# One head's last K tile taken in halves, and the output weights loaded wholly behind V, in a one-core decode kernel

## The chip, the cores and the metric

The kernel runs on one core of a Trainium2 chip. The metric is device time in microseconds; the figure for a kernel is the median of its runs.

## The reference

One token goes through cached attention and through a gated feed-forward network (FFN), and a gate mixes the two. There are 32 heads of 128 dimensions with 65536 keys each, the model width is 512 and the FFN's hidden width 1792. All inputs are bf16.

```python
x = A_x
g = _sigmoid((x * gate_w).sum(-1, keepdims=True))
# attention, per head h: q = x @ wq, p = softmax(q . k_cache[h] / sqrt(128)), o = p @ v_cache[h]; a = o @ wo
a = _A_ref(x, A_k_cache, A_v_cache, A_wq, A_wo)
# FFN: (silu(x @ w_gate) * (x @ w_up)) @ w_down
b = _B_ref(x, B_w_gate, B_w_up, B_w_down)
return g * a + (1 - g) * b
```

The K and V caches are 537 MB each, and each value is used once.

## The kernel before, in words

**Tiles.** A tile is 16384 keys of a head: 128 partitions with 128 keys of 128 values each (4 MB). Four tiles make a head, so there are 128 tiles of K and as many of V; they are numbered n = 0 to 127. Two tiles make a pair, numbered m = 0 to 63, which one transfer of 8 MB loads in most of the kernel. There are two K buffers of a pair each (`K_bufs`, used in turn) and one V buffer of a pair (`V_buf`), so a V pair can be loaded only after the value matmuls of the pair before it are done.

**Scores.** For a K tile, the vector engine DVE multiplies the keys in place by the query (`product`, L281) and adds the two halves of each key's 128 products (`add_halves` with `WIDE`, or `add_once`; L293 and L304). PE sums the 64 columns that are left: 16 matmuls of 512 columns against the identity (`scores`, L508) accumulate four partial sums per key in a PSUM bank (`S_ps`, one of two). DVE adds the four (`fold`, L315). In the long loop the second tile of each pair is added further on DVE, down to 16 columns (`T_sb`). When a head's four tiles are folded, DVE takes the maximum per partition (`row_max`, L321), PE and DVE find the maximum of all (`max_turn` L524, `top_of` L325), and ScalarE takes the exponentials of a pair at a time (`P_sb`).

**Values.** PE multiplies the exponentials with V, four keys of a partition per matmul: 32 matmuls per tile (`values`, L531). `head_turn` (L539) brings the result into one column per head, and ScalarE writes it, scaled, into `oT`. At the end `project` (L548) multiplies `oT` with `wo`: two matmuls of 256 columns per head, into `a_ps`.

**Order.** There is no scheduler: each engine's instructions stand in the order in which the code gives them, with hand-written semaphore waits. The sync engine (SP or SyncE) issues all large transfers from one queue and waits, between them, for the buffers that they overwrite.

**The prologue** (`prologue`) loads wq, then the first two K pairs (the first as two tiles), the FFN's gate and up weights, and, into places of `V_buf` that come free, the down weights; then the third K pair (L630, when tile 1's scores are done), the first V pair (L655, when the FFN's down projection has been read from `V_buf`) and the fourth K pair (L666, when tile 3's scores are done). DVE works on tiles 0 to 3, the first head; FFN work is put between them. After tile 2's add DVE waits for ScalarE's exponential of the FFN's gate (`eg`, L636), does four small operations on it, the last of which writes `hT`, and goes on to tile 3's product. On PE, in order: tile 2's scores, the 14 matmuls of the down projection from `hT` (L643), two matmuls that open `a_ps` with the FFN's part (L651), the spread of the second head's query (L521), tile 3's scores.

**The end** (`sync_end`, `tensor_end`). SP loads, after the last pair of head 30's V, the first 16 heads' rows of wo (2 MB, `EARLY`) into the first half of K buffer 0, then the last head's four V tiles: N-4 into the second half of K buffer 0, N-3 and N-2 into the V buffer's halves in two pieces each, N-1 into the second half of K buffer 1 in six pieces (`LAST_CUTS`), and then wo's other 16 heads into the first half of K buffer 1 in five pieces (`LATE_CUTS`). Heads below `GROUPED` (28) lie in rows of 4 KB, four heads to a row; heads 28 to 31 in rows of 1 KB. PE projects heads 0 to 15 in two portions around the `head_turn` of head 30, ahead of the last head's values, and heads 16 to 31 piece by piece behind them. The last 8 keys of a partition in the last tile (`TURNED`) go straight into the head's column (L745), so that `head_turn` of the last head only adds to it. Head 31's column is waited for ahead of its own two matmuls. DVE and ScalarE copy a half each of the result out, and SP stores it.

Of the kernel before, what the change touches and what calls it, by code (L numbers as in the profile page):

```python
# [8 lines left out]
ALU = mybir.AluOpType  # L9
AXIS = mybir.AxisListType  # L10
P = 128
NB = 128
PAIR = 2 * NB
QUAD = 4


WIDE = 64
WIDTH = 16

TURNED = 8  # L20
EARLY = 16
LATE_CUTS = (EARLY, 20, 24, 28, 30, 32)
HALVES = (0, 64, NB)
LAST_CUTS = (0, 32, 64, 96, 112, NB - TURNED, NB)

# [16 lines left out]
def kernel(  # L42
# [14 lines left out]
    nc = tc.nc  # L57
# [3 lines left out]
    _, H, Sk, Dh = A_k_cache.shape  # L61
    D = A_x.shape[2]
# [8 lines left out]
    HD = D // 2  # L71
# [13 lines left out]
    K_bufs = [ring.tile([P, PAIR * Dh], bf16, name=f"K{i}_buf") for i in range(2)]  # L85
# [9 lines left out]
    ident_b, ones_b, q_diag = (sb(n, [P, P], bf16) for n in ("ident_b", "ones_b", "q_diag"))  # L95
# [33 lines left out]

    K_half, V_half = [halves(b) for b in K_bufs], halves(V_buf)  # L130

    wo_sb = [b[:, : H * D].rearrange("p (h n) -> p h n", n=D) for b in K_bufs]

    def v_view(n):
        return {N - 4: K_half[0][1], N - 3: V_half[0], N - 2: V_half[1], N - 1: K_half[1][1]}[n]
# [17 lines left out]
        for n in ("x_in", "gw_in", "wq_in", "ka_in", "kb_in", "kc_in", "wg_in", "wu_in", "wd_in", "vA_in", "vB_in")  # L153
# [2 lines left out]
    v4_in = Events(nc, "v4_in", 16)  # L156
    end_in = {n: [Events(nc, f"end{n}_{i}", 16) for i in range(len(c) - 1)]
              for n, c in ((N - 3, HALVES), (N - 2, HALVES), (N - 1, LAST_CUTS))}
    wo_in = {a: Events(nc, f"wo{a}", 16) for a in (0, *LATE_CUTS[:-1])}

    c_S = [nc.alloc_semaphore(f"c_S{i}") for i in range(2)]
    c_q, c_P, c_V, c_o, c_m = (nc.alloc_semaphore(n) for n in ("c_q", "c_P", "c_V", "c_o", "c_m"))
# [5 lines left out]
    def wait(engine, events, value):  # L168
        key = id(engine), id(events)
        value -= taken.get(key, 0)  # L170
        if seen.get(key, 0) < value:
            engine.wait_ge(events.sem, value)
            seen[key] = value
# [12 lines left out]
        events(sync.dma_start(out=view[:, a:b, :], in_=rows_of(cache, n)[:, start + a : start + b, :]))  # L186

    def load_wo(a, b):
        runs = wo_sb[a >= EARLY].rearrange("p (g j) n -> p g (j n)", j=QUAD)
        rows = A_wo.rearrange("(h p) n -> p h n", p=P)  # L190
        row_runs = A_wo.rearrange("(g p j) n -> p g (j n)", p=P, j=QUAD)
        if b <= GROUPED:
            A, B = a // QUAD, b // QUAD
            wo_in[a](sync.dma_start(out=runs[:, A:B, :], in_=row_runs[:, A:B, :]))
        else:
            wo_in[a](sync.dma_start(out=wo_sb[1][:, a:b, :], in_=rows[:, a:b, :]))


    def load_v(i):
# [20 lines left out]

    def sync_end():
        wait(sync, pe_D, 6)
        load_wo(0, EARLY)
        load_tile(v_view(N - 4), A_v_cache, N - 4, v4_in)
        for n in (N - 3, N - 2, N - 1):
            if n < N - 1:
                wait(sync, pe_V, n - 2)
            else:
                wait(sync, pe_D, 8)
            cuts = LAST_CUTS if n == N - 1 else HALVES  # L230
            for events, a, b in zip(end_in[n], cuts[:-1], cuts[1:]):
                load_tile(v_view(n), A_v_cache, n, events, a, b)
        for a, b in zip(LATE_CUTS[:-1], LATE_CUTS[1:]):
            load_wo(a, b)

    def sync_out():
# [23 lines left out]

    own = [dv]

    def product(n):
        K = K_half[n // 2 % 2][n % 2]
        q = q_sb[n // G % 2]
        q_rep = bass.AP(tensor=q.tensor, offset=q[:, :].offset, ap=[list(q[:, :].ap[0]), [0, NB], [1, Dh]])
        m = n // 2

        if m == 0:
            wait(dve, (ka_in, kb_in)[n], 16)  # L270
        elif m == 1:
            wait(dve, kc_in, 16)
        elif n == N - 1:
            wait(dve, kb_in, 32)
        else:
            wait(dve, k_in[m % 2], 16 * (m // 2))
        if n < G:
            wait(dve, ac, marks["q"])
        else:
            wait(dve, ac_q, n // G)  # L280
        return own[0](dve.tensor_tensor(out=K, in0=K, in1=q_rep, op=ALU.mult))  # L281

    def add_halves(n, width, last, out=None, ahead=None):
        K = K_half[n // 2 % 2][n % 2]
        half, mark = Dh // 2, last
        while half >= width:
            wait(dve, own[0], mark)
            to = K[:, :, 0:half]
            if half == width and ahead is not None:
                fold(ahead)  # L290
            if half == width and out is not None:
                to = out
            ins = dve.tensor_tensor(out=to, in0=K[:, :, 0:half], in1=K[:, :, half : 2 * half], op=ALU.add)  # L293
            if half == width and out is not None:
                ins.then_inc(c_S[n % 2], 1)
            else:
                mark = own[0](ins)
            half //= 2
        marks["K", n] = mark

    def add_once(n, last):
        wait(dve, own[0], last)
# [200 lines left out]
        pe.wait_ge(credit, 1)  # L503
        pe.sem_inc(credit, -1)  # L504

    def scores(n, src, width, events):
        for c in range(0, width, QUAD):
            ins = pe.matmul(  # L508
                S_ps[n % 2], lhsT=ident_b, rhs=src[:, :, c : c + QUAD],
                start=(c == 0), stop=(c == width - QUAD),  # L510
            )
            if c == 0 and events is pe_S and n == 1:
                pe_K(ins)
        events(ins)

    def scores_direct(n):
        wait(pe, dv, marks["K", n])
        scores(n, K_half[n // 2 % 2][n % 2], WIDE, pe_D)

    def query_spread(events):  # L520
        events(pe.matmul(qb, lhsT=ones_b, rhs=q_diag, start=True, stop=True))  # L521
# [23 lines left out]
    def project(lo, hi):  # L545
        for h in range(lo, hi):
            for i, a in enumerate(a_ps):
                ins = pe.matmul(  # L548
                    a, lhsT=oT[:, h : h + 1], rhs=wo_sb[h >= EARLY][:, h, i * HD : (i + 1) * HD],
                    start=False, stop=(h == H - 1),  # L550
                )
                if h == H - 1:
                    pe_x(ins)


    def prologue():
# [76 lines left out]
        fold(1)  # L633
        add_halves(2, WIDE, last)
        scores_direct(2)
        wait(dve, ac, marks["eg"])  # L636
        wait(dve, dv, dv(dve.tensor_scalar_add(eg, eg, 1.0)))
        wait(dve, dv, dv(dve.reciprocal(eg, eg)))
        wait(dve, dv, dv(dve.tensor_tensor(out=hprod, in0=gu_sb[:, :FT], in1=eg, op=ALU.mult)))
        wait(pe, wd_in, 16)  # L640
        wait(pe, dv, dv(dve.tensor_tensor(out=hT, in0=hprod, in1=gu_sb[:, FT:], op=ALU.mult)))
        for t in range(FT):
            ins = pe.matmul(  # L643
                b_ps, lhsT=hT[:, t : t + 1], rhs=wd_sb[:, t, :], start=(t == 0), stop=(t == FT - 1)
            )
        pe_x(ins)
        wait(act, dv, marks["rest"])
        wait(act, pe_x, 4)
        wait(pe, ac, ac(copy(b_sb, b_ps, rest[0:1, :])))
# [8 lines left out]
        query_spread(pe_q0)  # L658
        wait(act, pe_q0, 2)
        ac_q(copy(q_sb[1], qb))  # L660
        last = product(3)
        fold(2)
        add_halves(3, WIDE, last)
        scores_direct(3)
        wait(sync, pe_D, 4)
        load_k(3)  # L666
        row_max(0, fold(3))
# [29 lines left out]
    def tensor_end():  # L697
        lower = P_sb[:, NB:]
        take(c_P)
        total()  # L700
        scores_direct(N - 4)
        take(c_V)
        pe_V(values(P_sb, V_half[0], 0, NB, True, False))
        scores_direct(N - 3)
        pe_V(values(lower, V_half[1], 0, NB, False, True))
        take(c_q)
        query_spread(pe_q)
        take(c_o)
        head_turn()
        take(c_m)  # L710
        max_turn()

        take(c_P)
        total()
        scores_direct(N - 2)
        take(c_V)
        pe_V(values(P_sb, V_half[0], 0, NB, True, False))
        scores_direct(N - 1)
        take(c_V)
        values(lower, V_half[1], 0, NB // 2, False, False)  # L720
        take(c_m)
        max_turn()
        pe_V(values(lower, V_half[1], NB // 2, NB, False, True))
        wait(pe, wo_in[0], 16)
        project(0, EARLY // 2)
        take(c_o)
        head_turn()
        project(EARLY // 2, EARLY)
        wait(pe, ac, marks["P_last"])
        wait(pe, v4_in, 16)  # L730
        pe_V(values(P_last, v_view(N - 4), 0, NB, True, False))
        for n in range(N - 3, N):
            probs = P_last[:, n % G * NB : (n % G + 1) * NB]
            cuts = LAST_CUTS if n == N - 1 else HALVES
            for events, a, b in zip(end_in[n], cuts[:-1], cuts[1:]):
                wait(pe, events, 16)
                if n == N - 1 and a == NB - TURNED:
                    break
                ins = values(probs, v_view(n), a, b, False, n == N - 1 and b == NB - TURNED)
            pe_V(ins)  # L740
            if n == N - 2:
                total(1)
        wait(pe, ac, marks["oh_read"])
        for j in range(NB - TURNED, NB):
            pe.matmul(  # L745
                oh, lhsT=v_view(N - 1)[:, j, :], rhs=probs[:, j : j + 1],
                start=(j == NB - TURNED), stop=False,
            )
        for a, b in zip(LATE_CUTS[:-1], LATE_CUTS[1:]):
            wait(pe, wo_in[a], 16)  # L750
            if a == EARLY:
                project(a, a + QUAD)
                wait(pe, ac, marks["O_last"])
                head_turn(opens=False)
                project(a + QUAD, b)
            elif b == H:
                project(a, H - 1)
                wait(pe, ac, marks["oT"])
                project(H - 1, H)
            else:  # L760
                project(a, b)

    with tc.tile_critical():
        prologue()
# [53 lines left out]
```

## Time and profile before

| | |
|---|---|
| median of 3 runs | 2520.32 us (2519.13 to 2520.52) |
| the profiled execution: its own time | 2520.22 us |
| its span, first to last instruction | 2518.4 us |
| mean granted TensorE clock | 0.774 |
| PE busy | 1485.8 us (59%) |
| DVE busy | 2003.5 us (80%) |
| ACT busy | 182.5 us (7%) |
| bytes read | 1087.64 MB, 432 GB/s over the span |

The profile is of one execution. Its views are a page (busy shares, the span in 40 slices, DMA queues, the costliest groups of instructions) and answers of the trace: timelines by engine, windows, waits. Times are microseconds from the first instruction. A timeline row gives the start, the length, the engine (SPq is SP's queue of transfers), the line of the kernel, the operation, the tiles written and read with shapes, a count, and in brackets how long the engine had been idle before and what released it. The rows of windows give start and end, the length, busy time and instruction count of PE, PE's weight loads, DVE, ACT and POOL, then the granted TensorE clock, the busy share of the 16 DMA engines, and GB/s. A large transfer is recorded in packets that are counted where they start, so a short window can show a share over 1 or of 0 although the engines are busy; windows are read together. "Time to landing" is from a transfer's issue to the event that all of its data are there.

### The profile page before, as it was taken

What the parts mean: (1) busy time and instruction counts of PE and PEld (TensorE: products, weight loads), DVE (VectorE), ACT (ScalarE), POOL (GpSimd) and SP (SyncE); (2) the same over time, 40 slices, a digit from 0 to 9 for tenths busy, and PEclk for the clock granted to TensorE, in tenths of its full rate; (3) what the DMA queues carried; (4) which work ended last, traced back from release to release, by engine and by line L of the source; (5) the groups of instructions that cost most, each with busy time, mean ns of one, the idle gap of its engine ahead of it and who ended that gap; (6) DMA issues with size and microseconds to landing.
All of it is one profiled execution on the core that took longest, in us unless ns stands there. A gap on an engine that the chain in (4) does not pass through costs nothing. (4 is left out here: it accounts for less than half of the span.)

```text
span 2518.4 us, 15666 instructions
## 1 busy us (share of the span) xinstructions
PE 1485.8 (59%) x6573; PEld 615.6 (24%) x6573; DVE 2003.5 (80%) x676; ACT 182.5 (7%) x503; POOL 0.7 (0%) x6
## 2 busy tenths in 40 slices
PE   2655646557556566465565564655755646557568
PEld 1322222222222222222222222222212222222223
DVE  5887877977878878779788787787887877977881
ACT  0000000000000000000000000000000000000000
POOL 0000000000000000000000000000000000000000
PEclk8777778778777787787787777877877778778789
DMA  9999999999999999999999999999999999999999
GB/s 413 424 432 432 433 433 433 434 433 434 433 433 433 433 433 435 439 438 434 433 433 434 434 433 433 433 433 433 433 435 438 438 434 434 433 434 434 433 429 388
DMA packets 22541, 1087.80 MB, mean 432 GB/s; under 512 B 2689, under 2 KB 3202, under 8 KB 4482
## 3 DMA queue, kind: packets, MB, share of 16 engines
q1 hardware_dynamic: 22242, 1087.65, 99.8%
q8 instruction: 7, 0.11, 0.0%
q10 hardware_dynamic: 288, 0.00, 0.0%
q14 instruction: 4, 0.03, 0.0%
HBM read 1087.64 MB, written 0.00 MB: 432 GB/s over the span
## 5 line engine op out<-in xcount | busy, mean ns | idle before, releaser
L281 DVE TENSOR_TENSOR K_buf<-K_buf,q_sb 128x16384 bf16<-128x16384 bf16 x128 | 1111.9, 8687 | 344.1 <-DMA K_buf<-in_A_k_cache_dram 344.1
L508 PE MATMUL S_ps<-K_buf,ident_b 128*128 128x512 bf16 x1088 | 387.2, 531 | 866.7 <-PEq L504 829.5
L531 PE MATMUL O_ps<-V_buf,P_sb 128*4 128x512 bf16 x3968 | 866.8, 379 | 31.8 <-PEq L504 31.4
L531 PEld LDWEIGHTS O_ps<-V_buf,P_sb 128*4 128x4 bf16 x3968 | 332.9, 85 | 563.3 <-issue 60.8
L293 DVE TENSOR_TENSOR K_buf<-K_buf 128x8192 bf16<-128x8192 bf16 (+1 forms) x128 | 438.2, 3423 | 3.1
L508 PEld LDWEIGHTS S_ps<-K_buf,ident_b 128*128 128x128 bf16 x1088 | 132.5, 126 | 1099.6 <-issue 1029.2
L304 DVE TENSOR_TENSOR K_buf<-K_buf 128x8192 bf16<-128x8192 bf16 x60 | 265.5, 4425 | 2.0
L387 ACT ACTIVATE O_sb<-O_ps 4x512 f32<-4x512 f32 x63 | 63.3, 1005 | 1705.2 <-PE qm_ps L521 1671.0
L315 DVE TENSOR_REDUCE S_sb<-S_ps 128x128 f32<-128x512 f32 x128 | 88.2, 689 | 110.3 <-PE S_ps L508 108.3
L524 PE MATMUL qm_ps<-diag,ones_f 128*128 128x128 f32 x126 | 34.0, 357 | 72.4 <-PEq L504 70.3
L539 PE MATMUL oh_ps<-ident_f,O_sb 4*128 4x1 f32 x504 | 64.3, 244 | 18.8 <-PEq L504 18.8
L293 DVE TENSOR_TENSOR T_sb<-K_buf 128x2048 bf16<-128x2048 bf16 x60 | 72.9, 1215 | 0.0
L539 PEld LDWEIGHTS oh_ps<-ident_f,O_sb 4*128 4x128 f32 x504 | 60.7, 186 | 48.7 <-issue 48.7
L508 PE MATMUL S_ps<-T_sb,ident_b 128*128 128x512 bf16 x240 | 64.7, 391 | 0.0
L524 PEld LDWEIGHTS qm_ps<-diag,ones_f 128*128 128x128 f32 x126 | 21.9, 218 | 76.7 <-issue 76.7
L387 ACT ACTIVATE bias<-top 128x1 f32<-128x1 f32 x32 | 6.5, 203 | 436.7 <-DVE top L325 436.7
L527 PE MATMUL tot_ps<-rs,ones_f 128*128 128x2 f32 (+1 forms) x126 | 24.5, 264 | 18.1 <-PEq L504 18.1
L387 ACT ACTIVATE oT<-whole_o,rg 32x1 f32 (+1 forms) x115 | 33.8, 294 | 4.7
L412 ACT ACTIVATE P_sb<-S_sb,bias 128x256 bf16<-128x256 f32 x62 | 31.5, 508 | 1.0
L527 PEld LDWEIGHTS tot_ps<-rs,ones_f 128*128 128x128 f32 x126 | 20.1, 200 | 36.9 <-issue 36.9
L334 DVE RECIPROCAL recip<-tot_ps 128x1 f32<-128x1 f32 x1 | 0.2, 169 | 32.0 <-PE tot_ps L527 32.0
L508 PEld LDWEIGHTS S_ps<-T_sb,ident_b 128*128 128x128 bf16 x240 | 20.7, 96 | 15.9
(61 smaller groups left out, 214.5 us busy)
## 6 DMA issues: line engine op xcount, KB each, us to landing
K_buf<-in_A_k_cache_dram SPq DMA_DIRECT2D x4, 4096.0 KB, 32.9
V_buf<-in_A_v_cache_dram SPq DMA_DIRECT2D x2, 4096.0 KB, 21.6
V_buf<-in_A_v_cache_dram SPq DMA_DIRECT2D x4, 2048.0 KB, 23.1
V_buf<-in_A_wq_dram SPq DMA_DIRECT2D x1, 4096.0 KB, 12.3
K_buf<-in_A_v_cache_dram SPq DMA_DIRECT2D x1, 4096.0 KB, 34.7
K_buf<-in_A_v_cache_dram SPq DMA_DIRECT2D x3, 1024.0 KB, 28.3
K_buf<-in_A_wo_dram SPq DMA_DIRECT2D x1, 2048.0 KB, 25.5
V_buf<-in_B_w_gate_dram SPq DMA_DIRECT2D x1, 1792.0 KB, 54.5
```

The costliest lines, as they stand in the source:

```text
L281: return own[0](dve.tensor_tensor(out=K, in0=K, in1=q_rep, op=ALU.mult))
L293: ins = dve.tensor_tensor(out=to, in0=K[:, :, 0:half], in1=K[:, :, half : 2 * half], op=ALU.add)
L304: dve.tensor_tensor(out=K[:, :, 0:half], in0=K[:, :, 0:half], in1=K[:, :, half:], op=ALU.add).then_inc(c_S[0], 1)
L315: return own[0](dve.tensor_reduce(out=S_sb[h % 2][:, g * NB : (g + 1) * NB], in_=S_ps[n % 2], axis=AXIS.X, op=ALU.add))
L334: wait(dve, own[0], own[0](dve.reciprocal(recip[:, 0:1], total)))
L387: return act.activation(out=out, in_=in_, func=ACT.Copy, scale=scale)
L412: return act.activation(out=out, in_=S_sb[h % 2][:, b * PAIR : b * PAIR + count], func=ACT.Exp, bias=bias[:, 0:1], scale=scale, accum_out= ...
L508: ins = pe.matmul(S_ps[n % 2], lhsT=ident_b, rhs=src[:, :, c : c + QUAD], start=(c == 0), stop=(c == width - QUAD),)
L524: pe.matmul(mT, lhsT=ones_f, rhs=diag, start=True, stop=True).then_inc(pe_m.sem, n)
L527: pe_t(pe.matmul(tot[:, :n], lhsT=ones_f, rhs=rs[:, :n], start=True, stop=True))
L531: ins = pe.matmul(O_ps, lhsT=probs[:, j : j + 4], rhs=view[:, j : j + 4, :], start=(opens and j == start), stop=(closes and j == stop - 4),)
L539: ins = pe.matmul(oh, lhsT=O_sb[:, c * Dh : (c + 1) * Dh], rhs=ident_f[0:4, c : c + 1], start=(opens and c == 0), stop=(c == 3),)
```

## The change

In the prologue, tile 3 of the first head is handled in two halves of 64 keys per partition. DVE's product of the first half stands ahead of the wait for the FFN gate's exponential, and its add behind the four gate operations; the second half's product, `fold(2)` and the second half's add follow. PE makes the first half's scores (16 matmuls of 256 columns) behind the down projection, ahead of the matmuls that open `a_ps`, and the second half's at the place where the whole tile's were. The event of tile 3's scores comes with the second half.

At the end, SP no longer loads 2 MB of wo ahead of the last head's V. All of wo (4 MB) goes into the first half of K buffer 0, behind V's last piece, in ten pieces (`WO_CUTS`): seven of four heads, one of two, two of one. PE has no projection ahead of the last head's values any more: it projects piece by piece behind them, with the last head's `head_turn` behind the first piece; the wait for head 31's column stands ahead of the last piece, which is that head alone.

```diff
-EARLY = 16
-LATE_CUTS = (EARLY, 20, 24, 28, 30, 32)
+WO_CUTS = (0, 4, 8, 12, 16, 20, 24, 28, 30, 31, 32)
...
-    wo_sb = [b[:, : H * D].rearrange("p (h n) -> p h n", n=D) for b in K_bufs]
+    wo_sb = K_bufs[0][:, : H * D].rearrange("p (h n) -> p h n", n=D)
...
     def sync_end():
         wait(sync, pe_D, 6)
-        load_wo(0, EARLY)
         load_tile(v_view(N - 4), A_v_cache, N - 4, v4_in)
...
-        for a, b in zip(LATE_CUTS[:-1], LATE_CUTS[1:]):
+        for a, b in zip(WO_CUTS[:-1], WO_CUTS[1:]):
             load_wo(a, b)
...
-    def product(n):
-        K = K_half[n // 2 % 2][n % 2]
+    def product(n, start=0, stop=NB):
+        K = K_half[n // 2 % 2][n % 2][:, start:stop, :]
...
+    def add_some(n, last, start, stop):
+        wait(dve, own[0], last)
+        K, half = K_half[n // 2 % 2][n % 2][:, start:stop, :], Dh // 2
+        marks["K", n] = own[0](dve.tensor_tensor(
+            out=K[:, :, 0:half], in0=K[:, :, 0:half], in1=K[:, :, half:], op=ALU.add
+        ))
...
-    def scores(n, src, width, events):
+    def scores(n, src, width, events, start=0, stop=NB):
         for c in range(0, width, QUAD):
             ins = pe.matmul(
-                S_ps[n % 2], lhsT=ident_b, rhs=src[:, :, c : c + QUAD],
+                S_ps[n % 2][:, start:stop, :], lhsT=ident_b, rhs=src[:, start:stop, c : c + QUAD],
...
-        events(ins)
+        if stop == NB:
+            events(ins)
...
         scores_direct(2)
+
+        first_half = product(3, 0, NB // 2)
         wait(dve, ac, marks["eg"])
...
         wait(pe, dv, dv(dve.tensor_tensor(out=hT, in0=hprod, in1=gu_sb[:, FT:], op=ALU.mult)))
+        add_some(3, first_half, 0, NB // 2)
...
         pe_x(ins)
+        scores_direct(3, 0, NB // 2)
         wait(act, dv, marks["rest"])
...
-        last = product(3)
+        last = product(3, NB // 2, NB)
         fold(2)
-        add_halves(3, WIDE, last)
-        scores_direct(3)
+        add_some(3, last, NB // 2, NB)
+        scores_direct(3, NB // 2, NB)
         wait(sync, pe_D, 4)
...
         pe_V(values(lower, V_half[1], NB // 2, NB, False, True))
-        wait(pe, wo_in[0], 16)
-        project(0, EARLY // 2)
         take(c_o)
         head_turn()
-        project(EARLY // 2, EARLY)
         wait(pe, ac, marks["P_last"])
...
-        for a, b in zip(LATE_CUTS[:-1], LATE_CUTS[1:]):
+        for a, b in zip(WO_CUTS[:-1], WO_CUTS[1:]):
             wait(pe, wo_in[a], 16)
-            if a == EARLY:
-                project(a, a + QUAD)
+            if b == H:
+                wait(pe, ac, marks["oT"])
+            project(a, b)
+            if a == 0:
                 wait(pe, ac, marks["O_last"])
                 head_turn(opens=False)
-                project(a + QUAD, b)
-            elif b == H:
-                project(a, H - 1)
-                wait(pe, ac, marks["oT"])
-                project(H - 1, H)
-            else:
-                project(a, b)
```

More of the change, by code (lines that the diff above doesn't have):

```diff
@@ L158 @@
               for n, c in ((N - 3, HALVES), (N - 2, HALVES), (N - 1, LAST_CUTS))}
-    wo_in = {a: Events(nc, f"wo{a}", 16) for a in (0, *LATE_CUTS[:-1])}
+    wo_in = {a: Events(nc, f"wo{a}", 16) for a in WO_CUTS[:-1]}
     c_S = [nc.alloc_semaphore(f"c_S{i}") for i in range(2)]
@@ L188, in load_wo @@
     def load_wo(a, b):
-        runs = wo_sb[a >= EARLY].rearrange("p (g j) n -> p g (j n)", j=QUAD)
+        runs = wo_sb.rearrange("p (g j) n -> p g (j n)", j=QUAD)
         rows = A_wo.rearrange("(h p) n -> p h n", p=P)
@@ L195, in load_wo @@
         else:
-            wo_in[a](sync.dma_start(out=wo_sb[1][:, a:b, :], in_=rows[:, a:b, :]))
+            wo_in[a](sync.dma_start(out=wo_sb[:, a:b, :], in_=rows[:, a:b, :]))
     def load_v(i):
@@ L261 @@
     own = [dv]
-    def product(n):
-        K = K_half[n // 2 % 2][n % 2]
+    def product(n, start=0, stop=NB):
+        K = K_half[n // 2 % 2][n % 2][:, start:stop, :]
         q = q_sb[n // G % 2]
-        q_rep = bass.AP(tensor=q.tensor, offset=q[:, :].offset, ap=[list(q[:, :].ap[0]), [0, NB], [1, Dh]])
+        q_rep = bass.AP(tensor=q.tensor, offset=q[:, :].offset, ap=[list(q[:, :].ap[0]), [0, stop - start], [1, Dh]])
         m = n // 2
@@ L513, in scores, with scores_direct @@
                 pe_K(ins)
-        events(ins)
-    def scores_direct(n):
+        if stop == NB:
+            events(ins)
+    def scores_direct(n, start=0, stop=NB):
         wait(pe, dv, marks["K", n])
-        scores(n, K_half[n // 2 % 2][n % 2], WIDE, pe_D)
+        scores(n, K_half[n // 2 % 2][n % 2], WIDE, pe_D, start, stop)
     def query_spread(events):
@@ L548, in project @@
                 ins = pe.matmul(
-                    a, lhsT=oT[:, h : h + 1], rhs=wo_sb[h >= EARLY][:, h, i * HD : (i + 1) * HD],
+                    a, lhsT=oT[:, h : h + 1], rhs=wo_sb[:, h, i * HD : (i + 1) * HD],
                     start=False, stop=(h == H - 1),
```

## The prediction

> **What bounds the kernel now.** I read the DMA view first: if the transfer engines never rest, only bytes or a hole in their stream can move the time.
>
> The DMA part of the page, 40 slices of 63 us:
>
> ```profile
> DMA  9999999999999999999999999999999999999999
> GB/s 413 424 432 432 433 433 433 434 433 434 433 433 433 433 433 435 439 438 434 433 433 434 434 433 433 433 433 433 433 435 438 438 434 434 433 434 434 433 429 388
> ...
> q1 hardware_dynamic: 22242, 1087.65, 99.8%
> q8 instruction: 7, 0.11, 0.0%
> ```
>
> One queue moves 1087.65 MB at some 433 GB/s from end to end. At that rate the bytes alone need 2512 us of the 2518.4. DVE (80% busy) and PE (59%) have slack, so an edit of the compute pays only where it closes a hole in the stream, or shortens what comes before the first byte or after the last. Only the first two slices and the last are under the plateau. Next, therefore, SyncE's rows (it issues all the big loads) and narrow windows of the start:
>
> ```profile
> 57.79 0.33 SPq L182 DMA_DIRECT2D K_buf<-in_A_k_cache_dram  x1
> 78.06 0.33 SPq L182 DMA_DIRECT2D V_buf<-in_A_v_cache_dram  x1
> 89.36 0.33 SPq L182 DMA_DIRECT2D K_buf<-in_A_k_cache_dram  x1
> 123.68 0.33 SPq L182 DMA_DIRECT2D V_buf<-in_A_v_cache_dram  x1
> ```
>
> Windows (the last two columns are DMA share and GB/s):
>
> ```profile
> 121.00:122.00 1.00, 1.00 (x7) 0.36 (x5) 0.27 (x1) 0.00 (x0) 0.00 (x0) 1.00 0.45 197
> 122.00:123.00 1.00, 1.00 (x6) 0.40 (x5) 0.00 (x0) 0.00 (x0) 0.00 (x0) 1.00 0.01 0
> 123.00:124.00 1.00, 1.00 (x8) 0.48 (x6) 0.00 (x0) 0.00 (x0) 0.00 (x0) 1.00 0.00 0
> ```
>
> There is one hole, from 122 to 124.6 us. The fourth K pair has run out and the second V pair is issued only at 123.68, because V has one buffer and the first V pair's 64 value matmuls (13.97 us from 109.68) end then. No other stretch up to the last byte shows such a hole. So the chain that ends in those value matmuls costs time. I followed it back on DVE:
>
> ```profile
> 62.37 4.42 DVE L293 TENSOR_TENSOR K_buf<-K_buf 128x8192 bf16<-128x8192 bf16 x1
> 69.12 0.18 DVE L637 TENSOR_SCALAR eg<-eg 128x14 f32<-128x14 f32 x1 [2.33 <-ACT eg L628]
> ...
> 69.91 8.69 DVE L281 TENSOR_TENSOR K_buf<-K_buf,q_sb 128x16384 bf16<-128x16384 bf16 x1
> ...
> 89.36 0.69 DVE L315 TENSOR_REDUCE S_sb<-S_ps 128x128 f32<-128x512 f32 x1 [5.84 <-PE S_ps L508]
> 90.09 0.69 DVE L321 TENSOR_REDUCE m<-S_sb 128x1 f32<-128x512 f32 x1
> 90.69 8.68 DVE L281 TENSOR_TENSOR K_buf<-K_buf,q_sb 128x16384 bf16<-128x16384 bf16 x1
> ```
>
> Two rests lie on the chain: 2.33 us for the FFN's exponential, and 5.84 us in which PE makes the last tile's scores. Last, the end, PE and then DVE:
>
> ```profile
> 2510.92 1.03 PE L548 MATMUL a_ps<-K_buf,oT 128*1 128x256 bf16 x8 [0.31 <-DMA K_buf<-in_A_wo_dram]
> 2511.89 1.05 PE L539 MATMUL oh_ps<-ident_f,O_sb 4*128 4x1 f32 x8
> 2512.86 2.78 PE L548 MATMUL a_ps<-K_buf,oT 128*1 128x256 bf16 x24
> 2515.57 0.41 DVE L383 CAST out_sb<-a_ps 1x256 bf16<-1x256 f32 x1 [11.50 <-PE a_ps L548]
> ```
>
> The last wo piece lands at 2500.2 + 14.5 = 2514.7 (issue plus time to landing), yet the output copy starts 0.85 us later, since PE is still in its run of 24 projection matmuls.
>
> **The change, the start.** By the order listing, DVE does: add of tile 2, product of tile 3's keys 0-63, the four gate operations, add of that half, product of keys 64-127, fold(2), add of the second half.
> Per operation, start to start, a whole product is 8.60 us, a whole add 4.34, a fold 0.60, the gate operations 0.79; halves of the first two are taken as 4.30 and 2.17. From the add's end at 66.7: first product to 71.0, gate to 71.8, add to 74.0, product to 78.3, fold to 78.9, add to 81.1, where before it ended at 83.45. DVE gains its rest, 2.35 us; nothing is added but some 0.1 us for two more instructions.
> The gate operations end 1.9 us later (71.8 for 69.9). Behind hT on PE are the 14 down-projection matmuls, which start at 74.85 anyway, after tile 2's scores: covered by 3 us, so the first V load (waiting for them at 78.06) doesn't move.
> PE then makes the first half's scores, 16 matmuls of 256 columns, from 78.06. Before these, 256 columns were only seen with a one-column weight (0.119 us each); 512 columns against the same weights took 0.227 at clock 1.0 and 0.43 at 0.5. So 16 cost between 1.8 and 6.9 us; I take 2 to 3.5, near half the 512-column price, as the stream sets it. Queued behind them are the two a_ps openers and the spread of query 1 (1.3 us together, with their ACT copy): they move from 78.9 to some 81, and query 1 is first read by tile 4's product.
> The second half's scores: from 81.2 for 2 to 3.5 us (bounds 1.8 and 6.9), so 83.2 to 84.8 (88.1 at worst) for 89.36 before. SyncE's load of the fourth K pair goes out with it; the queue is full then, so that is worth nothing by itself. Then fold and row maximum, 1.3 us. Now the next thing is late: tile 4's product waits for its K pair, which lands at 57.79 + 27.7 = 85.5. It starts at 85.5 to 86.2 for 90.69: 4.5 to 5.2 us earlier. Scores of tile 4 then start at 98.7 to 99.4 for 103.98, and, at the half clock in which they begin, end near 105.5. The first V pair lands at 78.06 + 26.7 = 104.8. So the value matmuls run from 105.6 to 119.6, and the second V pair is issued near 119.6, 2.5 us ahead of the dry queue; data followed an issue at 123.68 by 1 us (first packets at 124.64), so 1.5 us is spare.
> What the hole is worth: in the trace's packets thirteen of the sixteen DMA engines end the K pair by 122.3 and three at 123.5 to 123.8; all start again at 124.64 and the first packets take some 3.2 us for 2.42. The slowest engine's loss is the spacing of landings, 145.3 - 124.2 = 21.1 us for 19.3 between later pairs: 1.8. The first engine's is longer: its packets end at 122.27 and 144.9, so 22.6 less 19.3: 3.3. Each of the three late engines was held up by one 16 KB instruction packet (queue 8), and the hole lets the others wait for them. Which engine is last at the end differs from those, as far as lateness shows there (a 1.7 us spread after three further such packets), so I take 3.0. Later, V issues come 3.5 us ahead of the dry queue (199.37 against 202.9), so no new hole follows.
>
> **The change, the end.** SyncE no longer issues wo's first 2 MB ahead of V; V lands 4.87 us earlier against the stream, wo's last byte as before: the bytes are the same. PE loses 32 projection matmuls (2 x 1.91 us) between its value blocks and gets all 64 behind V. Value blocks of 32 take 6.72 us, and V arrives at 9.7 us a block: PE ends V at about 2505.3 in old times, and wo's pieces come 1.21 to 1.24 us apart (landings of the three 512 KB pieces) against 0.95 us for eight matmuls. PE catches up after the head turn (1.0 us) by the sixth piece. At the last piece only two matmuls are left: the copies start near 2515.25 for 2515.57. Worth 0.3 us. The five added DMAs: 0.02 us each for 512 KB pieces (1.23 for 1.21 by bytes), 0.1 for the 1 KB rows of heads 28 to 31 (0.70 for 0.60 by bytes): 0.1 in all, counted in that 0.3. Bounds: -0.3 to +0.6.
> The Trainium skill (DMA: Bandwidth & Descriptors, Anatomy of one DMA) gives a fixed cost of about 2.0 us per DMA beside the bytes, and its rules for kernel authors ask for 1 MiB or more per DMA; by that, unhidden, the cut would cost 10 us, while the rows just named show 1.23 us between whole 512 KB pieces.
>
> Sum: 3.0 + 0.3 = 3.3 us. Span 2518.4 to 2515.1; the profiled execution 2520.22 to 2516.9; the median stands 0.1 above it: **2517.0**.
>
> **The rivals.**
> *The late engine stays late (17%).* If the engine that ends last is one of the three held up at the start, only the 1.8 comes back: with the tail's 0.3, 2518.2. For it: lateness persists for hundreds of us when no hole evens it out. Against it: only some of 16 engines.
> *The hole stays (8%).* If scores at half clock take the 512-column price, or the clock comes late in the value matmuls, the V issue is not before 122 and the start gives little: 2520.0 with the tail's 0.3.
> *PE becomes the bound of the end (slower, 3%).* The place is the 64 projection matmuls behind V. They fall behind the pieces when eight cost over 1.21 us, that is at a granted clock under 0.79. At 0.5 each takes 0.107 us more, 6.8 in all: less the 3.3, 2523.8; if the last V tile's 30 matmuls run so too (0.21 more each) 2530. Against it: the clock is 1.0 from 2453 to the end, with waits of over 1 us in it, and PE's longest new wait is 1.4 us. In the Trainium skill (TensorE: Matmul & The Clock Gate, Part 1) the clock halves after an idle window of about 3.4 us, which no wait here reaches; the trace's clock fell at 128.9 after PE went idle near 127.5, so it can be quicker.
> *The pieces pay their start each (slower, 2%).* If a piece's fixed time is not hidden by the one ahead, each of five costs about the 2.1 us of the 1 KB load of x (page, part 6): 10.5 - 3.3, so 2527.5. It decides only when the queue is empty between pieces; SyncE issued the last ones 14.5 us ahead.
> That the edit doesn't do what it says is out for the order of instructions, which is listed as described.
>
> **How the numbers follow.** The forecast has 70%, 2517.0, its own range 2516 to 2518. The 80% range takes in the late engine with 0.6 us of spread between runs (2519.13 to 2520.52 before): 2515.8 to 2519.1; the hole that stays and the slower cases are left out. About 0.2%, 5.0 us, is what a measurement here can tell from no change. Faster by that would need 1.7 us more than forecast, over the hole's and the tail's bounds together (3.3 + 0.6): 3%. Slower by that: the pieces, and the clock's worse half: 4%. The rest, 93%, is within.
>
> **What would show it.** Right: no DVE wait at the gate; the 5.84 us rest under 4; tile 4's product ending a wait for DMA near 85.5; the second V pair issued near 119.6; no window without bytes near 122; copies 0.5 us after the last wo landing; the span 3 us shorter. Wrong: a V issue after 121.3; a wait on PE for wo shorter than expected with matmuls of 0.21 us; wo pieces more than 1.3 us apart.

## The result and the profile after

The changed kernel takes 2516.34 us (median of 22 runs, 2515.96 to 2518.0) where the kernel before, run beside it, takes 2520.23 (22 runs, 2518.9 to 2521.85): 3.9 us less, ratio 0.9985 with a 95% interval of 0.9979 to 0.9990. The forecast was 2517.0. The profiled execution took 2517.20 us, 0.9 above the median, with a span of 2515.4.

First the stream, from the page of the changed kernel; then SyncE's rows and the three windows around the hole of before, of which 122 to 124 us had no bytes then (columns as in the windows of the prediction):

```profile
GB/s 414 438 433 436 435 434 434 434 434 434 435 434 434 434 434 434 435 436 435 435 435 434 437 434 435 435 434 437 435 434 434 434 434 434 434 435 434 434 431 387
```

```profile
57.58 0.33 SPq L181 DMA_DIRECT2D K_buf<-in_A_k_cache_dram  x1
77.86 0.33 SPq L181 DMA_DIRECT2D V_buf<-in_A_v_cache_dram  x1
83.26 0.33 SPq L181 DMA_DIRECT2D K_buf<-in_A_k_cache_dram  x1
119.12 0.33 SPq L181 DMA_DIRECT2D V_buf<-in_A_v_cache_dram  x1
```

```profile
121.00:122.00 1.00, 0.80 (x8) 0.74 (x7) 0.00 (x0) 0.23 (x2) 0.00 (x0) 1.00 0.92 393
122.00:123.00 1.00, 0.75 (x4) 0.51 (x4) 0.00 (x0) 0.77 (x3) 0.00 (x0) 1.00 1.65 655
123.00:124.00 1.00, 0.00 (x0) 0.00 (x0) 0.00 (x0) 0.00 (x0) 0.00 (x0) 1.00 0.46 197
```

The second slice went from 424 to 438 GB/s, and the first and last stand as they did. The second V pair is issued at 119.12 us for 123.68, while the fourth K pair is still landing, so bytes move through 122 to 124. The pair after the hole now lands 24.2 us after its issue, at 143.3, 19.3 us behind the K pair (83.26 + 40.7 = 124.0), which is the distance of undisturbed pairs; before it was 21.1.

DVE of the changed kernel, from tile 2's add to tile 4's product:

```profile
62.38 4.42 DVE L291 TENSOR_TENSOR K_buf<-K_buf 128x8192 bf16<-128x8192 bf16 x1
66.72 4.42 DVE L279 TENSOR_TENSOR K_buf<-K_buf,q_sb 128x8192 bf16<-128x8192 bf16 x1
71.05 0.17 DVE L645 TENSOR_SCALAR eg<-eg 128x14 f32<-128x14 f32 x1
...
71.83 2.28 DVE L302 TENSOR_TENSOR K_buf<-K_buf 128x4096 bf16<-128x4096 bf16 x1
74.03 4.42 DVE L279 TENSOR_TENSOR K_buf<-K_buf,q_sb 128x8192 bf16<-128x8192 bf16 x1
...
83.27 0.69 DVE L320 TENSOR_REDUCE S_sb<-S_ps 128x128 f32<-128x512 f32 x1 [2.02 <-PE S_ps L513]
83.99 0.69 DVE L326 TENSOR_REDUCE m<-S_sb 128x1 f32<-128x512 f32 x1
85.41 8.69 DVE L279 TENSOR_TENSOR K_buf<-K_buf,q_sb 128x16384 bf16<-128x16384 bf16 x1 [0.73 <-DMA K_buf<-in_A_k_cache_dram]
```

The gate's operations no longer wait, the rest for PE is 2.02 us for 5.84, and tile 4's product ends a wait for its K pair at 85.41, 5.3 us earlier than before. The end, PE and DVE:

```profile
2503.29 1.03 PE L554 MATMUL a_ps<-K_buf,oT 128*1 128x256 bf16 x8 [0.21 <-DMA K_buf<-in_A_wo_dram]
2504.26 1.05 PE L545 MATMUL oh_ps<-ident_f,O_sb 4*128 4x1 f32 x8
2505.24 2.79 PE L554 MATMUL a_ps<-K_buf,oT 128*1 128x256 bf16 x24
2508.23 1.03 PE L554 MATMUL a_ps<-K_buf,oT 128*1 128x256 bf16 x8 [0.21 <-DMA K_buf<-in_A_wo_dram]
...
2510.73 1.91 PE L554 MATMUL a_ps<-K_buf,oT 128*1 128x256 bf16 x16 [0.21 <-DMA K_buf<-in_A_wo_dram]
```

```profile
2512.56 0.41 DVE L388 CAST out_sb<-a_ps 1x256 bf16<-1x256 f32 x1 [16.73 <-PE a_ps L554]
```

PE has caught up by the fifth piece and then waits 0.21 us for a piece at a time. The trace has the last wo piece landed at 2512.05, so the copy comes 0.51 us behind it; before it came 0.83 us behind (2514.74).

### The profile page after: what moved, and what is told of

The parts are those of the page before. It is cut to its first block, busy times and chain, and to the rows that moved or that the text cites. A ratio compares the mean times of both kernels' runs of the same rounds, so it can differ in the third digit from the quotient of the medians.

```text
span 2515.4 us, 15705 instructions
## 1 busy us (share of the span) xinstructions
PE 1487.4 (59%) x6589; PEld 616.2 (24%) x6589; DVE 2003.4 (80%) x678; ACT 182.3 (7%) x503; POOL 0.7 (0%) x6
## 5 line engine op out<-in xcount | busy, mean ns | idle before, releaser
L279 DVE TENSOR_TENSOR K_buf<-K_buf,q_sb 128x16384 bf16<-128x16384 bf16 (+1 forms) x129 | 1112.0, 8620 | 348.8 <-DMA K_buf<-in_A_k_cache_dram 346.1
L513 PE MATMUL S_ps<-K_buf,ident_b 128*128 128x512 bf16 (+1 forms) x1104 | 388.9, 527 | 867.3 <-PEq L509 834.3
L291 DVE TENSOR_TENSOR K_buf<-K_buf 128x4096 bf16<-128x4096 bf16 (+1 forms) x127 | 433.7, 3415 | 3.1
L320 DVE TENSOR_REDUCE S_sb<-S_ps 128x128 f32<-128x512 f32 x128 | 88.2, 689 | 105.4 <-PE S_ps L513 103.3
L326 DVE TENSOR_REDUCE m<-S_sb 128x1 f32<-128x512 f32 x32 | 22.0, 686 | 1.1
```

The source lines that it names most:

```text
L320: return own[0](dve.tensor_reduce(out=S_sb[h % 2][:, g * NB : (g + 1) * NB], in_=S_ps[n % 2], axis=AXIS.X, op=ALU.add))
L513: ins = pe.matmul(S_ps[n % 2][:, start:stop, :], lhsT=ident_b, rhs=src[:, start:stop, c : c + QUAD], start=(c == 0), stop=(c == width - QUAD),
```

## The experiments

Each of the first seven kernels (called e1 to e7 here) was timed 11 times, beside runs of the kernel before: median 2520.41 us for e1 to e4, 2520.43 for e5 to e7. The intervals of these ratios are some 0.09% to either side, 2.3 us, so differences of less than that rest on the traces.

**One part at a time.** The start alone (e1) is the kernel before with the diff's prologue part, the end alone (e2) the changed kernel with the old prologue.

```diff
 # e1: the kernel before, with the prologue's part of the change (product, add_some, scores, scores_direct)
+        first_half = product(3, 0, NB // 2)
...
 # e2: the changed kernel without it
-        first_half = product(3, 0, NB // 2)
...
+        last = product(3)
```

> The kernel before with the prologue's change alone (tile 3 in halves around the gate's operations); the end is as before. Forecast's theory (the hole in the stream near 122 us is what the change closes, worth 3.0 us): 3.0 us less than before, near 2517.2 us, second V pair issued near 119 us, no window without bytes near 122. Rival, the late engine stays late: 1.8 us less, near 2518.4. Rival, the gain is at the end: within 0.5 us of before.

> The kernel before with the end's change alone (all of wo behind V in ten pieces); the prologue is as before. Forecast's theory: PE has two matmuls left at the last piece, worth 0.3 us, near 2519.9 us; the hole near 122 us stays, second V pair issued at 123.7. Rival, the 0.6 us by which the change did better than forecast lies here: 0.9 us less than before, near 2519.3. Rival, each added piece costs DMA time: slower than before.

The start alone took 2516.68 us (ratio 0.9986, 0.9977 to 0.9995), 3.7 less than before; the end alone 2519.93 (1.0000, 0.9991 to 1.0009), 0.5 less by its median, which its interval doesn't tell from nothing. SyncE's second V issue, in the start alone and then in the end alone:

```profile
119.06 0.33 SPq L182 DMA_DIRECT2D V_buf<-in_A_v_cache_dram  x1
```

```profile
123.78 0.33 SPq L181 DMA_DIRECT2D V_buf<-in_A_v_cache_dram  x1
```

The gain goes with that issue: the rival that it lies at the end would leave the start alone within 0.5 us of before, and the interval allows 1.3 to 5.8 us less. The 1.8 us of the late engine lie inside that interval, but in the profiles the last wo piece landed 3.7 us earlier than before (2511.03 for 2514.74). What the end does shows in the traces: last landing to output copy 0.83 us in the start alone, 0.48 in the end alone (2514.80 to 2515.28). The time of the profiled execution is 5.47 to 5.51 us more than its last landing in all seven profiles with the old end, and 5.10 to 5.15 in all five with the new end in ten pieces: 0.35 us. By this the rival that the end held the missing 0.6 us falls. A price of pieces doesn't show in the time, within the interval.

**The wait moved, nothing halved (e3).** One line of the kernel before is moved.

```diff
         scores_direct(2)
+        last = product(3)
         wait(dve, ac, marks["eg"])
...
-        last = product(3)
         fold(2)
```

> The kernel before with one line moved: DVE's whole product of tile 3 stands ahead of the wait for the FFN gate's exponential, the four gate operations behind it; nothing is halved and the end is as before. Forecast's theory: DVE gains its rest of 2.3 us, hT comes at 76.1 us (the first V load at 79.3, still ahead of the dry queue), tile 3's scores end at 87.0 to 87.9 for 89.36, second V pair issued at 121.3 to 122.2: most of the hole closed, 2 to 3 us less than before, 2517.2 to 2518.2. Rival, the halves on PE are what counts: under 1 us less.

It took 2517.41 us (0.9989, 0.9980 to 0.9998), 3.0 less than before, and issued the second V pair at 119.38, some 2 us earlier than the theory had it; bytes moved where the hole had been:

```profile
119.38 0.33 SPq L182 DMA_DIRECT2D V_buf<-in_A_v_cache_dram  x1
```

```profile
122.00:123.00 1.00, 0.58 (x5) 0.44 (x4) 0.00 (x0) 0.96 (x4) 0.00 (x0) 1.00 2.09 852
```

The reason for the early issue is in tile 3's scores. First PE's rows and a window of this kernel, then the same of the kernel before (PE's clock is the third number from the end of a window):

```profile
76.34 3.18 PE L644 MATMUL O_ps<-V_buf,hT 128*1 128x512 bf16 x14 [1.83 <-DVE hT L642]
80.36 1.02 PE L652 MATMUL a_ps<-O_sb,ones_f 1*1 1x256 f32 x4 [0.83 <-ACT O_sb L387]
81.31 0.23 PE L521 MATMUL qm_ps<-q_diag,ones_b 128*128 128x128 bf16 x1
81.38 3.62 PE L508 MATMUL S_ps<-K_buf,ident_b 128*128 128x512 bf16 x16
```

```profile
82.00:84.00 2.00, 2.00 (x11) 0.88 (x10) 0.00 (x0) 0.00 (x0) 0.00 (x0) 1.00 1.21 524
```

```profile
83.58 5.74 PE L508 MATMUL S_ps<-K_buf,ident_b 128*128 128x512 bf16 x16 [3.54 <-DVE K_buf L293]
```

```profile
82.00:84.00 2.00, 0.42 (x2) 0.14 (x3) 1.53 (x1) 0.00 (x0) 0.00 (x0) 0.50 1.21 524
```

The same 16 matmuls of 512 columns took 3.62 us for 5.74. In the kernel before PE rested 3.54 us ahead of them, and its granted clock stepped down to 0.5 at 81.1, 1.0 us into that rest; here PE had no rest ahead of the scores, and the clock stayed at 1.0 until 87.0, 2.0 us behind their end. That the rest brought the step is argued from these two, not shown. So the move alone closed the hole; halving was not needed for that. The same start with the changed kernel's end (e7):

> The end of the changed kernel with the simpler start of the earlier run (DVE's whole product ahead of the gate's wait, nothing halved). Theory: the hole is closed already and the halves add nothing, so the time is that of the changed kernel within 0.5 us, 2516.3 to 2516.9. Rival, the halves are worth the 0.7 us by which the simpler start alone was behind the halves alone (2517.41 for 2516.68): 2517.0 or more.

2517.07 us (0.9988, 0.9979 to 0.9997), with the V issue at 119.85: on time, like the changed kernel's. Its median is 0.7 us above the changed kernel's, as the rival had it, but that is within the intervals, and the profile of neither kernel shows a hole. Whether the halves are worth anything beside the move stays open; the single times below bear on it.

**The chain made longer (e4, e5).** Folds of tile 3, which change no result, are repeated on DVE ahead of the row maximum.

```diff
         load_k(3)
+        for _ in range(3):      # 8 in the second kernel
+            wait(dve, dv, fold(3))
         row_max(0, fold(3))
```

> The changed kernel with three more folds of tile 3 (some 0.73 us each, one behind the other, 2.2 us in all) on DVE ahead of the row maximum. Forecast's theory (only the dry queue counts, and the second V pair's issue at 119.1 has 2.2 us to spare): tile 4's product had waited 0.7 us for its K pair, so the issue moves by 1.5 us to 120.6, and the time stays within 0.3 us of the changed kernel, 2516.3. Rival, the prologue's chain itself sets the time: 1.5 to 2.2 us more, 2517.8 to 2518.5.

> The changed kernel with eight more folds of tile 3 on DVE ahead of the row maximum (some 0.73 us each): tile 4's product then starts near 90.4 us, where it started in the kernel before, while the halves, the early fourth K load and the new end all stay. Theory of the hole: the second V pair is issued near 123.5 us again, the windows near 122 to 124 are without bytes again, and the start's gain is lost: 2519.6 to 2520.0 us, as with the new end alone (2519.93). Rival, the early load of the fourth K pair or the halves are worth something by themselves: under 2518.

Three folds: 2516.84 us (0.9989, 0.9980 to 0.9998), 0.5 above the changed kernel and not told from it by the median; the profile shows no hole. Tile 4's scores in the changed kernel and then here:

```profile
98.71 6.48 PE L513 MATMUL S_ps<-K_buf,ident_b 128*128 128x512 bf16 x16 [12.99 <-PEq L509]
```

```profile
100.20 5.26 PE L513 MATMUL S_ps<-K_buf,ident_b 128*128 128x512 bf16 x16 [11.85 <-PEq L509]
```

The V issue moved by 0.3 us only (119.39), not by 1.5: the scores started 1.5 us later but ended within 0.3 us of each other, since they begin at half clock and the clock's step up, at 103.6 here and 104.5 there, falls into them. Part of that is luck of this one profile: at 0.43 us a matmul before the step and 0.227 behind it, a start 1.5 us later costs an estimated 0.8 us with the step in the same place, and the step that came 1.0 us earlier gave some 0.5 of it back. So the spare time ahead of the dry queue was tried by 0.3 us here, not by 1.5. Eight folds: 2519.64 us (0.9999, 0.9990 to 1.0008), 3.3 above the changed kernel though the halves, the early K load and the new end are all there. DVE, SyncE and the windows of that run:

```profile
83.44 6.49 DVE L320 TENSOR_REDUCE S_sb<-S_ps 128x128 f32<-128x512 f32 x9 [2.02 <-PE S_ps L513]
89.97 0.69 DVE L326 TENSOR_REDUCE m<-S_sb 128x1 f32<-128x512 f32 x1
90.57 8.68 DVE L279 TENSOR_TENSOR K_buf<-K_buf,q_sb 128x16384 bf16<-128x16384 bf16 x1
```

```profile
122.90 0.33 SPq L181 DMA_DIRECT2D V_buf<-in_A_v_cache_dram  x1
```

```profile
121.00:122.00 1.00, 1.00 (x6) 0.41 (x5) 0.15 (x1) 0.00 (x0) 0.00 (x0) 1.00 0.45 197
122.00:123.00 1.00, 1.00 (x7) 0.37 (x5) 0.00 (x0) 0.00 (x0) 0.00 (x0) 1.00 0.01 0
123.00:124.00 1.00, 1.00 (x7) 0.39 (x6) 0.00 (x0) 0.70 (x1) 0.00 (x0) 1.00 1.19 393
```

With tile 4's product back at 90.57 us (90.69 before) the V issue is late again, the window from 122 is empty again, and the start's gain is gone. The issue came at 122.90 for the 123.5 expected, so the hole is a little shorter than before. This is the experiment that shows the hole as the cause: 2.2 us of added work, which left the issue in time, cost nothing that the median tells, and 5.8 us, which made it late, cost 3.3.

**Fewer pieces (e6).** wo behind V in four pieces.

```diff
-WO_CUTS = (0, 4, 8, 12, 16, 20, 24, 28, 30, 31, 32)
+WO_CUTS = (0, 28, 30, 31, 32)
```

> The changed kernel with wo in four pieces behind V for ten (heads 0 to 27 in one piece, then 28 and 29, 30, 31). If pieces cost DMA time, the last piece lands earlier by what six pieces cost (0.1 us by the forecast's rows, up to 12 us if each paid 2.1). If the cuts serve to hide PE's projection: heads 0 to 27 land near 2510.7 us, PE then has 56 matmuls of 0.119 us, the head turn of 1.0 us and 8 matmuls more ahead of it, so the output copies come at 2519.3 for 2512.6: 6.5 us more than the changed kernel, near 2522.9.

2524.65 us (1.0019, 1.0010 to 1.0028): 8.3 more than the changed kernel, 4.2 more than the kernel before. PE, then three windows:

```profile
2510.05 8.09 PE L554 MATMUL a_ps<-K_buf,oT 128*1 128x256 bf16 x56 [7.77 <-DMA K_buf<-in_A_wo_dram]
2518.07 1.05 PE L545 MATMUL oh_ps<-ident_f,O_sb 4*128 4x1 f32 x8
2519.05 1.03 PE L554 MATMUL a_ps<-K_buf,oT 128*1 128x256 bf16 x8
```

```profile
2504.00:2506.00 2.00, 0.00 (x0) 0.00 (x0) 0.00 (x0) 0.00 (x0) 0.00 (x0) 1.00 1.01 418
...
2508.00:2510.00 2.00, 0.00 (x0) 0.00 (x0) 0.00 (x0) 0.00 (x0) 0.00 (x0) 0.50 0.90 335
...
2514.00:2516.00 2.00, 2.00 (x20) 1.53 (x19) 0.00 (x0) 0.00 (x0) 0.00 (x0) 1.00 0.00 0
```

The cuts hide the projection. All of wo was there at 2511.3, and the copies came at 2520.0. The 56 matmuls took 8.0 us where 56 times 0.119 makes 6.7, because PE had rested 7.77 us and began them at half clock: the clock fell at 2507.0, 4.7 us into the rest, and was back at 2513.8. The expectation (some 6.5 us more, with PE at full clock) lacked this; in the profiles the copies came 7.5 us later. The Trainium skill (TensorE: Matmul & The Clock Gate, Part 1) has the clock halve after an idle window of about 3.4 us. These windows agree with that, but the steps at 81.1 in the kernel before and at 87.0 in e3 came 1.0 and 2.0 us into a rest; if the rests brought those steps, a much shorter one is enough here. What the pieces cost the stream can't be read from these two profiles: the DMA engine that was first done with the last piece was done 0.38 us earlier here than in the changed kernel (2509.23 for 2509.61), but the middle one of the sixteen 0.26 us later (2510.65 for 2510.39).

**The spread of the simpler start.** Its 11 times lay between 2516.4 and 2519.8 us, so the kernel of e3 was profiled four times more (e8a to e8d).

> The kernel with DVE's whole product ahead of the gate's wait again, profiled once more, because its 11 times spread over 2516.4 to 2519.8 us where the changed kernel's kept to 2516.0 to 2518.0. Theory (PE's clock doubles at a step that falls differently in each execution, so tile 4's scores, and with them the second V pair's issue, end at different times around the dry queue): a run with the issue under 121.3 us takes 2516.4 to 2517.5, and each us of issue beyond that adds one. Rival, the transfer engines' lateness at the end makes the spread: the issue is at 119.4 in every run.

> A second look at the same kernel: time over 2517.5 us only with an issue later than 121.3 us, by the clock's step; by the rival, with the issue at 119.4.

> A third look at the same kernel, with the same expectations.

> A fourth look at the same kernel, with the same expectations.

They took 2517.26, 2517.77, 2516.54 and 2516.33 us (the kernel before 2519.69 once, beside them), with the V issue at 119.60, 119.78, 118.99 and 118.71: all on time. The theory had an issue after 121.3 behind the time over 2517.5, and it wasn't there. The last landings are at 2511.78, 2512.30, 2511.07 and 2510.82, in the order of the times, and they lie 1.5 us apart where those of the middle engine lie 0.5 apart (2510.31 to 2510.82). That speaks for the rival, lateness of the last engine. But the issues are in the same order too, though all in time, and four runs don't separate the two.

None of the times over 2518.0 us was met, so what is behind those stays open. They are not spread evenly: the start alone and the changed kernel, whose profiles issue the second V pair at 119.1, have none in 33 runs, and e3, e7 and the three folds, whose profiles issue it at 119.4 to 119.9, have 10 in 33. So the longer chain, and the move without the halves, may cost something in some executions that the medians and these profiles don't show.

## Why the prediction was right

**The bound.** One hole in an otherwise full stream: shown, by taking it away in three ways (e1, e3 and the change) and by putting most of it back (e5). Averaged over the sixteen DMA engines, the second V pair landed 22.3 us behind the fourth K pair in the kernel before and in the end alone, 21.5 with eight folds, and 19.3 to 19.7 in all other profiles.

**DVE's steps.** Forecast 71.0, 71.8, 74.0, 78.3, 78.9 for the starts behind the halves, measured 71.05, 71.83, 74.03, 78.37, 78.97. The gate's operations ended later and the first V load went out at 77.86 (78.06 before): covered, as argued.

**PE's halves.** Taken as 2 to 3.5 us each; they took 1.93 each, since the clock stayed at 1.0. The upper end, half of 16 times 0.43, was the price at half clock, which the kernel before had in that place. The next step hid most of that error: tile 4's product was ready at 84.7 and waited for its K pair in any case. Forecast 85.5 to 86.2, measured 85.41.

**The V issue.** Forecast 119.6, measured 119.12; tile 4's scores ended at 105.1 for 105.5.

**The hole's worth.** Forecast 3.0 us, between 1.8 for the last DMA engine and 3.3 for the first. In the landings of the last wo piece the middle engine (the ninth of sixteen) came from 2513.42 to 2510.39: 3.0. The medians gave more for the start alone, 3.7, with an interval of 1.3 to 5.8 us, so the term was not shown to be wrong. The profile of the start alone shows what can make such a difference: there the last wo piece landed 3.7 us earlier than before, 3.1 of it at the middle engine, the rest because its last engine was less late. *The late engine stays late* did not come about as a loss, but lateness did move the ends: in the changed kernel's profile the last engine was 1.66 us behind the middle one, in the start alone 0.67, before 1.32. It fits that the profiled execution of the changed kernel lies 0.9 above its median, and that of the start alone (2516.50) 0.2 below its own. Over all the profiles this lateness was 0.34 to 1.66 us; the forecast had no way to know it, so agreement closer than some 1 us is luck.

**The end.** Forecast 0.3 us from PE's shorter last run; measured 0.32 in the two profiles (0.83 to 0.51), 0.35 over all of them, and 0.5 by medians in the end alone, which its interval doesn't tell from nothing. Pieces landed 1.21 to 1.26 us apart, as forecast.

**The rivals.** *The hole stays*: out. *The pieces pay their start each*: out, by the landings, which came 1.21 to 1.26 us apart for 1.21 by bytes. The 2.0 us that the prediction quotes from the Trainium skill (DMA: Bandwidth & Descriptors, Anatomy of one DMA) is given there for transfers issued from GpSimd. SyncE issues the pieces here. *PE becomes the bound of the end* did not happen, since from the last head's V on PE's waits for transfers were 0.6 us at the longest; but e6 showed its mechanism at work, an idle PE that starts a projection at half clock, once the pieces were too large.

## What to carry to other kernels

Where a transfer queue is full nearly everywhere, look for the one place where it runs dry and follow back what its next issue waited for; work on that chain is worth time until the issue comes before the queue is empty; beyond that the medians here show no gain, though the times over 2518 us warn that some spare may be wanted. A cheap operation that waits should stand behind long work that is ready: moving one line did most of it here. Data that PE must still work on after the last byte was best cut so that the work on each piece was shorter than the next piece's transfer; then PE's waits stayed at 0.2 us and its clock at 1.0, where the uncut data cost it a rest of 7.77 us and half its clock.

## What was not expected of the hardware

A shift of work on PE changed its price: the same 16 matmuls took 5.74 us, begun at half clock behind a rest of 3.54 us, and 3.62 at full clock without the rest. And a later start moved the end by less: scores that began at 98.71 and at 100.20 us, both at half clock, ended at 105.1 and 105.4, because the clock's step up fell into them, and came 1.0 us earlier in the run that began later.
